# One hand-written order of stages on every engine, in a linear-attention and SoLU kernel

## The chip, the cores and the metric

The kernel runs on one core of a Trainium2 chip. A core has a matrix engine (PE), a vector engine (DVE), an activation engine (ACT), a general engine (POOL), an engine that mostly starts transfers (SP), and 16 DMA engines. Each engine works through its own queue strictly in order, and the engines wait for one another through semaphores. Matrix results land in PSUM, everything else lies in SBUF. The metric is the time of one execution in device microseconds (us).

## What is computed

Two operations run one after the other. The first is a linear attention with a decaying state, for 4 batches, 8 heads, 768 steps and 48 values a head. The second takes its 3072 x 384 result through a two-layer block with a SoLU activation and a layer norm.

```python
for t in range(S):                       # r, k, v, w: (4, 8, 768, 48); u: (8, 48)
    cur = einsum('bhd,bhe->bhde', u[None] * kt, vt)
    y[:, :, t] = einsum('bhd,bhde->bhe', rt, state + cur)
    state = wt[:, :, :, None] * state + einsum('bhd,bhe->bhde', kt, vt)

h = x @ w_in                             # (3072, 384) @ (384, 1024)
sm = softmax(h)                          # over the 1024
solu = h * sm
ln = (solu - mean(solu)) / sqrt(var(solu) + 1e-06) * g_ln
out = ln @ w_out                         # (3072, 1024) @ (1024, 384)
```

## The kernel before

The work is cut into 24 units: 6 chunks of 128 steps, and within each chunk the 4 batches. A unit passes these stages, each a function of the kernel:

- `load`: four tiles (w, k, r, v) of 128 x 384 f32, 192 KB each, started on SP. Each name has 5 buffers.
- `decay`: ACT takes the logarithm of w (tile lw, L128), PE sums it over time into cum_ps (L130, L131), ACT takes the exponential in place (L132).
- `scaled`: DVE forms kp and rp from it (L139, L140). `bonus`: POOL forms vb, p, q and dv, and DVE sums q into dg (L146 to L154).
- `transposed`: PE transposes kp and rp into kr_ps, DVE copies it to kr (L164). `scores`: PE forms m_ps from kr, ACT copies it to m (L176), POOL masks it (L177).
- `attend`: PE sums y_ps from dv, the state st and m times vb; ACT copies it to y (L196). `state`: PE forms s_ps, ACT its decay et (L221), DVE the new st of that batch (L226).
- `x_transposed`: PE transposes y into x_ps, DVE copies it to xT (L235). `hidden`: 24 matmuls form h_ps (L244), ACT takes e = exp(h_ps) (L247), DVE forms he = h_ps * e (L249).
- `output`: 24 matmuls, in eight groups of three, form o_ps (he times w2), g_ps (he times he) and a last column of o_ps (L259 to L262). ACT squares the sums (sq), DVE takes the diagonal of g_ps (junk, L268), POOL subtracts (qm, L270), ACT forms lv, rs and the scaled result o (L272 to L276), and SP stores o.

`setup_weights`, called once, folds the norm's scale and mean into w2: sixteen f32 matmul instructions over w_out and gn (L115), then eight sums on DVE (L119).

The loop at the end of the kernel works on units t, t - 1, t - 2, t - 3 and t - 4 at once. It is not this loop alone that sets the order on the engines: a scheduler moves instructions of different stages past each other by its own estimate of costs, and PSUM and SBUF buffers are handed out in the order that it finds. PSUM has two buffers of tag "b" (cum_ps, m_ps, h_ps), and four of tag "s" (kr_ps, s_ps, x_ps, y_ps, o_ps, g_ps).

Of the kernel before, what the change touches and what calls it, by code (L numbers as in the profile page):

```python
# [16 lines left out]
MULT, ADD = ALU.mult, ALU.add  # L17


@with_exitstack  # L20
def kernel(
# [23 lines left out]
    NU = len(units)  # L45

# [55 lines left out]
    nc.sync.dma_start(out=g_sb, in_=moe_g_ln.rearrange("(ko ki) -> ki ko", ki=128))  # L102
    w2 = consts.tile([128, KF, DM + 1], BF16)

    def setup_weights():

        gr = consts.tile([128, KF], F32)
        nc.vector.tensor_scalar(out=gr, in0=g_sb, scalar1=RDF, scalar2=None, op0=MULT)
        gn = consts.tile([128, KF, 128], F32)
        nc.gpsimd.memset(gn, -1.0 / DF)  # L110
        for f in range(KF):
            nc.vector.tensor_scalar(out=gn[:, f, :], in0=gn[:, f, :], scalar1=gr[:, f:f + 1], scalar2=None, op0=MULT)
        m_ps = small.tile([128, DM], F32, tag="s", name="m_ps")
        for f in range(KF):
            nc.tensor.matmul(m_ps, lhsT=gn[:, f, :], rhs=wout_f[:, f, :], start=(f == 0), stop=(f == KF - 1))  # L115
        m_sb = consts.tile([128, DM], F32)
        nc.vector.tensor_copy(out=m_sb, in_=m_ps)
        for f in range(KF):
            nc.vector.scalar_tensor_tensor(out=w2[:, f, :DM], in0=wout_f[:, f, :], scalar=gr[:, f:f + 1],  # L119
                                           in1=m_sb, op0=MULT, op1=ADD)  # L120
        nc.vector.memset(w2[:, :, DM:], 1.0 / RDF)


    def decay(i):
        L = live[i]
        lw = lw_t[i % NR]
        L["lw"] = lw
        nc.scalar.activation(out=lw[:, :, :D], in_=L["w"], func=LN)  # L128
        cum = big.tile([C, 2, 512], F32, tag="b", name="cum_ps")
        nc.tensor.matmul(cum[:, 0, :DM], lhsT=uti_neg, rhs=lw[:, :, :D], start=True, stop=True)  # L130
        nc.tensor.matmul(cum[:, 1, :DM], lhsT=uts, rhs=lw[:, :, :D], start=True, stop=True)  # L131
        nc.scalar.activation(out=cum[:, :, :DM], in_=cum[:, :, :DM], func=EXP)  # L132
        L["ex"] = cum

    def scaled(i):
# [3 lines left out]
        nc.vector.tensor_mul(out=kp[:, :, :D], in0=ex[:, 0], in1=L["k"])  # L139
        nc.vector.tensor_mul(out=rp[:, :, :D], in0=ex[:, 1], in1=L["r"])  # L140
        L["kp"], L["rp"] = kp, rp

    def bonus(i):
        L = live[i]
        vb = wk.tile([C, H, D], BF16, tag="vb", name="vb")
        nc.gpsimd.tensor_copy(out=vb, in_=L["v"])  # L146
        p = wk.tile([C, H, D], BF16, tag="p", name="p")
        nc.gpsimd.tensor_mul(out=p, in0=L["r"], in1=L["k"])  # L148
        q = wk.tile([C, H, D], BF16, tag="q", name="q")
        nc.gpsimd.tensor_mul(out=q, in0=p, in1=u_bc)  # L150
        dg = wk.tile([C, H], F32, tag="dg", name="dg")
        nc.vector.reduce_sum(out=dg, in_=q, axis=AX)  # L152
        dv = wk.tile([C, H, D], BF16, tag="dv", name="dv")
        nc.gpsimd.tensor_mul(out=dv, in0=vb, in1=dg.unsqueeze(2).to_broadcast([C, H, D]))  # L154
        L["vb"], L["dv"] = vb, dv

    def transposed(i):
        L = live[i]
        kr_ps = small.tile([C, 2 * HP, C], BF16, tag="s", name="kr_ps")
        for j, t in ((0, L["kp"]), (1, L["rp"])):  # L160
            for hp in range(HP):
                nc.tensor.transpose(kr_ps[:, j * HP + hp, :], t[:, 2 * hp:2 * hp + 2, :].rearrange("t a d -> t (a d)"), ident)  # L162
        kr = wk.tile([C, 2 * HP, C], BF16, tag="kr", name="kr")
        nc.vector.tensor_copy(out=kr, in_=kr_ps)  # L164
        L["kr"] = kr

    def scores(i):
# [3 lines left out]
        for hp in range(HP):  # L171
            for a in range(2):
                rows = slice(64 * a, 64 * a + 64)
                nc.tensor.matmul(m_ps[:, a, hp, :], lhsT=kr[rows, hp, :], rhs=kr[rows, HP + hp, :], start=True, stop=True)  # L174
        m = wk.tile([C, 2, HP, C], BF16, tag="m", name="m")
        nc.scalar.copy(out=m, in_=m_ps)  # L176
        nc.gpsimd.affine_select(out=m, in_=m, compare_op=ALU.is_gt, fill=0.0, base=0,  # L177
                                pattern=[[0, H], [1, C]], channel_multiplier=-1)
        L["m"] = m

    def attend(i):
# [4 lines left out]
        nc.tensor.matmul(y_ps, lhsT=ident, rhs=L["dv"].rearrange("t h d -> t (h d)"), start=True, stop=False,  # L186
                         skip_group_check=True)
        if c > 0:
            for hp in range(HP):
                nc.tensor.matmul(y_ps[:, hp * 2 * D:(hp + 1) * 2 * D], lhsT=kr[:, HP + hp, :], rhs=st[:, hp, :],  # L190
                                 start=False, stop=False, skip_group_check=True)
        for h in range(H):
            nc.tensor.matmul(y_ps[:, h * D:(h + 1) * D], lhsT=m[:, h % 2, h // 2, :], rhs=vb[:, h, :],
                             start=False, stop=(h == H - 1), skip_group_check=True)
        y = wk.tile([C, DM], BF16, tag="y", name="y")
        nc.scalar.copy(out=y, in_=y_ps)  # L196
        L["y"] = y

    def state(i):
# [7 lines left out]
        if c > 0:  # L207
            nc.tensor.matmul(s_ps[:, :DM], lhsT=ident, rhs=st.rearrange("p a e -> p (a e)"), start=True, stop=False,
                             skip_group_check=True)
# [12 lines left out]
        sv = s_ps[:, :DM].rearrange("p (a e) -> p a e", a=HP)
        for a in range(2):
            rows = slice(64 * a, 64 * a + 64)
            cols = slice(a * D, (a + 1) * D)
            nc.vector.tensor_mul(out=st[rows, :, cols], in0=sv[rows, :, cols],  # L226
                                 in1=et[rows].unsqueeze(2).to_broadcast([64, HP, D]))

    def x_transposed(i):
        L = live[i]  # L230
        x_ps = small.tile([128, KM, C], BF16, tag="s", name="x_ps")
        for j in range(KM):
            nc.tensor.transpose(x_ps[:, j, :], L["y"][:, j * 128:(j + 1) * 128], ident)
        xT = wk.tile([128, KM, C], BF16, tag="xT", name="xT")
        nc.vector.tensor_copy(out=xT, in_=x_ps)  # L235
# [3 lines left out]
    def hidden(i):  # L239
        L = live[i]  # L240
        h_ps = big.tile([128, KF, C], F32, tag="b", name="h_ps")
        for f in range(KF):
            for j in range(KM):
                nc.tensor.matmul(h_ps[:, f, :], lhsT=win_sb[:, j, f * 128:(f + 1) * 128], rhs=L["xT"][:, j, :],  # L244
                                 start=(j == 0), stop=(j == KM - 1))
        e = wk.tile([128, KF, C], BF16, tag="e", name="e")
        nc.scalar.activation(out=e, in_=h_ps, func=EXP)  # L247
        he = wk.tile([128, KF, C], BF16, tag="he", name="he")
        nc.vector.tensor_mul(out=he, in0=h_ps, in1=e)  # L249
        L["e"], L["he"] = e, he  # L250

    def output(i):
        L = live[i]
        c, b = units[i]
        e, he = L["e"], L["he"]
        o_ps = small.tile([C, DM + 2], F32, tag="s", name="o_ps")
        g_ps = small.tile([C, C], F32, tag="s", name="g_ps")
        for f in range(KF):
            nc.tensor.matmul(o_ps[:, :DM + 1], lhsT=he[:, f, :], rhs=w2[:, f, :], start=(f == 0), stop=False,  # L259
                             skip_group_check=True)  # L260
            nc.tensor.matmul(g_ps, lhsT=he[:, f, :], rhs=he[:, f, :], start=(f == 0), stop=(f == KF - 1))  # L261
            nc.tensor.matmul(o_ps[:, DM + 1:], lhsT=e[:, f, :], rhs=inv_col, start=False, stop=(f == KF - 1),  # L262
                             skip_group_check=True)
        sq = wk.tile([C, 2], F32, tag="sq", name="sq")
        nc.scalar.activation(out=sq, in_=o_ps[:, DM:], func=SQUARE)
        junk = wk.tile([C, C], BF16, tag="junk", name="junk")
        ss = wk.tile([C, 1], F32, tag="ss", name="ss")
        nc.vector.scalar_tensor_tensor(out=junk, in0=g_ps, scalar=1.0, in1=ident, op0=MULT, op1=MULT, accum_out=ss)  # L268
        qm = wk.tile([C, 1], F32, tag="qm", name="qm")
        nc.gpsimd.tensor_sub(out=qm, in0=ss, in1=sq[:, 0:1])  # L270
        lv = wk.tile([C, 1], F32, tag="lv", name="lv")
        nc.scalar.activation(out=lv, in_=sq[:, 1:2], func=LN, scale=1e-6 * DF * DF, bias=qm)  # L272
# [6 lines left out]
    LOOK = 3
    for i in range(2, LOOK):  # L280
        load(i)
    LAST = 5
    for t in range(NU + LAST):
        on = lambda d: 0 <= t - d < NU
        if t + LOOK < NU:
            load(t + LOOK)
        if on(0):
            decay(t)
            bonus(t)
        if on(3):  # L290
            hidden(t - 3)
        if on(0):
            scaled(t)
        if on(1):
            transposed(t - 1)
        if on(2):
            attend(t - 2)
        if on(4):
            output(t - 4)
        if on(1):  # L300
            scores(t - 1)
        if on(2):
            x_transposed(t - 2)
            state(t - 2)
        if t == 1:
            setup_weights()
# [30 lines left out]
```

## Time and profile before

| What | Value |
|---|---|
| median of 3 runs | 202.47 us (201.85 to 202.66) |
| the profiled execution's own time | 202.66 us |
| its span, first to last instruction | 201.0 us |
| busy: PE / DVE / ACT / POOL | 149.8 / 118.7 / 113.3 / 110.3 us |
| moved by DMA | 26.51 MB, of it 101312 packets under 512 bytes |
| DMA engines | 5 to 9 tenths busy in nearly every slice until 150 us, 0 to 2 tenths after, when all loads have landed |

How to read the rows of a profile: a row of the timeline gives the start (us from the span's start), the length, the engine, the line of the kernel, the operation, the tile written and the tiles read, the shape, and in brackets how long the engine stood idle before it and what it waited for. "x24" at the end says that 24 instructions are merged. A matmul's own length overlaps the next one's start, so PE's pace is read from start to start. A row of the busy time by stretches gives the stretch and its length, the busy time of PE, weight loads, DVE, ACT and POOL (with numbers of instructions), the granted PE clock, the DMA engines' busy share and GB/s. In the page's clock row each digit is a fortieth of the span, in tenths of full speed.

### The profile page before, as it was taken

To read this page: it belongs to the slowest core of one execution; us is meant where nothing else is said; L and a number is where in the kernel's file an instruction comes from. 1 tells how busy PE (TensorE), PEld (TensorE's weight loads), DVE (VectorE), ACT (ScalarE), POOL (GpSimd) and SP (SyncE) were. 2 spreads that over 40 slices of the span, in tenths; PEclk is the share of its full clock that TensorE was granted. 3 is DMA by queue.
4 is the path that set the end of the run, shared out by engine and by line. 5 is a ranking of instruction groups with operands and counts; after the bars stand their busy time and mean duration, and the time that the engine had idled before them with its cause. 6 is when DMAs were issued, how large, how long until landed. Compare 5 with 4: busy or idle time off the path is not lost.

```text
span 201.0 us, 5426 instructions
## 1 busy us (share of the span) xinstructions
PE 149.8 (75%) x2144; PEld 117.3 (58%) x2144; DVE 118.7 (59%) x266; ACT 113.3 (56%) x237; POOL 110.3 (55%) x156
## 2 busy tenths in 40 slices
PE   1031394389869797968788988899888988999870
PEld 0010253278757676756676867677776867786650
DVE  3032418959775576668378676777677666663320
ACT  3042103057754775767577677766867677765642
POOL 4046566378754974873986577656865245411200
PEclk9999999559999999999999999999999999999997
DMA  6999799995196799678979597678640111011112
GB/s 115 210 188 297 148 192 186 187 174 109 53 186 151 152 175 205 125 135 171 194 159 159 131 218 151 134 160 175 143 112 10 44 39 42 3 39 42 39 42 80
DMA packets 105946, 26.51 MB, mean 132 GB/s; under 512 B 101312, under 2 KB 105536, under 8 KB 105920
## 3 DMA queue, kind: packets, MB, share of 16 engines
q1 hardware_dynamic: 105520, 25.37, 65.4%
q0 software_dynamic: 400, 0.79, 2.1%
q8 instruction: 17, 0.28, 0.6%
q14 instruction: 9, 0.07, 0.1%
HBM read 22.22 MB, written 4.72 MB: 134 GB/s over the span
## 4 chain that ended last, share of the span: by engine, by line
PE 27%; ACT 15%; issue 14%; DVE 13%; POOL 12%; DMA 11%; SPq 6%; POOLq 0%; DVEq 0%
PE h_ps L244 10%; DMA r_in<-in_r_dram 7%; ACT e L247 6%; SPq L62 5%; DMA g_sb<-in_moe_g_ln_dram 5%; PE o_ps L259 5%; PE m_ps L115 4%; DVE he L249 3%; DVE w L119 3%; POOL m L177 3%; ACT lw L128 3%; DVE junk L268 2%; POOL p L148 2%; POOL q L150 2%; PE cum_ps L130 2%
## 5 line engine op out<-in xcount | busy, mean ns | idle before, releaser
L259 PE MATMUL o_ps<-w,he 128*128 128x385 bf16 x192 | 49.2, 324 | 1.1 <-DVE he L249 1.1
L261 PE MATMUL g_ps<-he 128*128 128x128 bf16 x192 | 41.6, 218 | 0.0
L249 DVE TENSOR_TENSOR he<-h_ps,e 128x1024 bf16<-128x1024 f32 x24 | 29.3, 1221 | 15.8 <-ACT e L247 15.8
L244 PEld LDWEIGHTS <-win_sb 128*128 128x128 bf16 x576 | 35.3, 100 | 4.1 <-issue 1.4
L244 PE MATMUL h_ps<-xT,win_sb 128*128 128x128 bf16 x576 | 37.2, 223 | 0.5 <-ACT m L176 0.5
L262 PE MATMUL o_ps<-inv_col,e 128*128 128x1 bf16 x192 | 31.9, 166 | 0.0
L247 ACT ACTIVATE e<-h_ps 128x1024 bf16<-128x1024 f32 x24 | 24.6, 1023 | 12.5 <-PE h_ps L244 12.4
L270 POOL TENSOR_TENSOR qm<-ss,sq 128x1 f32<-128x1 f32 x24 | 4.5, 190 | 48.5 <-DVE junk L268 48.5
L148 POOL TENSOR_TENSOR p<-r_in,k_in 128x384 bf16<-128x384 f32 x24 | 24.4, 1016 | 9.1 <-DMA r_in<-in_r_dram 9.1
L176 ACT CAST m<-m_ps 128x1024 bf16<-128x1024 f32 x24 | 24.0, 999 | 9.5 <-PE m_ps L174 9.3
L177 POOL TENSOR_SCALAR_AFFINE_SELECT m<-m 128x1024 bf16<-128x1024 bf16 x24 | 26.2, 1091 | 3.9 <-ACT m L176 3.9
L130 PE MATMUL cum_ps<-lw,uti_neg 128*128 128x384 bf16 x24 | 8.2, 343 | 25.0 <-ACT lw L128 25.0
L262 PEld LDWEIGHTS <-e 128*128 128x128 bf16 x192 | 18.4, 96 | 12.5
L139 DVE TENSOR_TENSOR kp<-cum_ps,k_in 128x384 bf16<-128x384 f32 x24 | 13.4, 557 | 20.5 <-ACT cum_ps L132 20.4
L152 DVE TENSOR_REDUCE dg<-q 128x8 f32<-128x384 bf16 x24 | 13.3, 552 | 19.7 <-POOL q L150 15.3
L132 ACT ACTIVATE cum_ps<-cum_ps 128x768 f32<-128x768 f32 x24 | 19.1, 797 | 9.8 <-PE cum_ps L131 7.7
L150 POOL TENSOR_TENSOR q<-p,u_bc 128x384 bf16<-128x384 bf16 x24 | 22.2, 925 | 3.5 <-DMA u_bc<-in_u_dram 1.8
L154 POOL TENSOR_TENSOR dv<-vb,dg 128x384 bf16<-128x384 bf16 x24 | 19.8, 828 | 5.4 <-DVE dg L152 4.3
L164 DVE COPY kr<-kr_ps 128x1024 bf16<-128x1024 bf16 x24 | 16.6, 690 | 8.6 <-PE kr_ps L162 8.3
L128 ACT ACTIVATE lw<-w_in 128x384 bf16<-128x384 f32 x24 | 12.5, 520 | 15.6 <-DMA w_in<-in_w_dram 15.1
L146 POOL CAST vb<-v_in 128x384 bf16<-128x384 f32 x24 | 12.2, 507 | 15.4 <-DMA v_in<-in_v_dram 7.9
L259 PEld LDWEIGHTS <-he 128*128 128x128 bf16 x192 | 18.6, 97 | 1.3 <-DVE he L249 1.2
(61 smaller groups left out, 274.8 us busy)
## 6 DMA issues: line engine op xcount, KB each, us to landing
w_in<-in_w_dram SPq DMA_DIRECT2D x24, 192.0 KB, 4.2
k_in<-in_k_dram SPq DMA_DIRECT2D x24, 192.0 KB, 3.9
r_in<-in_r_dram SPq DMA_DIRECT2D x24, 192.0 KB, 4.1
v_in<-in_v_dram SPq DMA_DIRECT2D x24, 192.0 KB, 4.1
out_dram<-o SPq DMA_DIRECT2D x24, 192.0 KB, 2.0
wout_f<-in_moe_w_out_dram SPq DMA_DIRECT2D x1, 1536.0 KB, 9.7
win_sb<-in_moe_w_in_dram POOLq DMA_DIRECT2D x1, 768.0 KB, 7.8
u_bc<-in_u_dram SPq DMA_DIRECT2D x1, 192.0 KB, 6.3
```

The costliest lines, as they stand in the source:

```text
L132: nc.scalar.activation(out=cum[:, :, :DM], in_=cum[:, :, :DM], func=EXP)
L148: nc.gpsimd.tensor_mul(out=p, in0=L["r"], in1=L["k"])
L150: nc.gpsimd.tensor_mul(out=q, in0=p, in1=u_bc)
L154: nc.gpsimd.tensor_mul(out=dv, in0=vb, in1=dg.unsqueeze(2).to_broadcast([C, H, D]))
L176: nc.scalar.copy(out=m, in_=m_ps)
L177: nc.gpsimd.affine_select(out=m, in_=m, compare_op=ALU.is_gt, fill=0.0, base=0, pattern=[[0, H], [1, C]], channel_multiplier=-1)
L244: nc.tensor.matmul(h_ps[:, f, :], lhsT=win_sb[:, j, f * 128:(f + 1) * 128], rhs=L["xT"][:, j, :], start=(j == 0), stop=(j == KM - 1))
L247: nc.scalar.activation(out=e, in_=h_ps, func=EXP)
L249: nc.vector.tensor_mul(out=he, in0=h_ps, in1=e)
L259: nc.tensor.matmul(o_ps[:, :DM + 1], lhsT=he[:, f, :], rhs=w2[:, f, :], start=(f == 0), stop=False, skip_group_check=True)
L261: nc.tensor.matmul(g_ps, lhsT=he[:, f, :], rhs=he[:, f, :], start=(f == 0), stop=(f == KF - 1))
L262: nc.tensor.matmul(o_ps[:, DM + 1:], lhsT=e[:, f, :], rhs=inv_col, start=False, stop=(f == KF - 1), skip_group_check=True)
```

## The change

Each of PE, ACT, DVE and POOL is wrapped in `InOrder`, which ties every instruction to the one written before it on the same engine. The scheduler can no longer move instructions on these four engines; SP is not wrapped. The stages are cut into a part for each engine (`log_w`, `cumulate`, `decays`, ...), and the new loop writes them out, from t + 1 (logarithm, bonus, cum, scaled) to t - 4 (store). `output` is called in two parts of four groups each. w_in is loaded in f32 through SP ahead of unit 1's tiles and cast on DVE at t = 1; w_out is scaled and centred in bf16 at t = 3, with eight bf16 matmuls and one sum over all of it on DVE. In the profile of the changed kernel nearly all instructions carry the helper's line, L34, so tiles tell them apart.

```diff
+class InOrder:
...
+        def call(*args, **kwargs):
+            if self.last is None:
+                made = make(*args, **kwargs)
+            else:
+                with self.tc.issue_after(self.last):
+                    made = make(*args, **kwargs)
+            self.last = made.ins
+            return made
...
+    pe, act, dve, pool = (InOrder(tc, e) for e in (nc.tensor, nc.scalar, nc.vector, nc.gpsimd))
...
-    load(1)
     u_bc = consts.tile([C, H, D], F32)
     nc.sync.dma_start(out=u_bc, in_=u.partition_broadcast(C))
-    win_sb = consts.tile([128, KM, DF], BF16)
-    nc.gpsimd.dma_start(out=win_sb, in_=moe_w_in.rearrange("(ko ki) f -> ki ko f", ki=128))
+    win_f = consts.tile([128, KM, DF], F32)
+    nc.sync.dma_start(out=win_f, in_=moe_w_in.rearrange("(ko ki) f -> ki ko f", ki=128))
+    load(1)
     wout_f = consts.tile([128, KF, DM], F32)
     nc.sync.dma_start(out=wout_f, in_=moe_w_out.rearrange("(ko ki) d -> ki ko d", ki=128))
...
+    load(2)
...
+    def setup_w_in():
+        for j in range(KM):
+            dve.tensor_copy(out=win_sb[:, j, :], in_=win_f[:, j, :])
+
+    def setup_w_out():
...
+        gw = consts.tile([128, KF, DM], BF16)
         for f in range(KF):
-            nc.vector.tensor_scalar(out=gn[:, f, :], in0=gn[:, f, :], scalar1=gr[:, f:f + 1], scalar2=None, op0=MULT)
-        m_ps = small.tile([128, DM], F32, tag="s", name="m_ps")
+            dve.tensor_scalar(out=gw[:, f, :], in0=wout_f[:, f, :], scalar1=gr[:, f:f + 1], scalar2=None, op0=MULT)
+        m_ps = small.tile([128, DM], F32, tag="s", name="mean_ps")
         for f in range(KF):
-            nc.tensor.matmul(m_ps, lhsT=gn[:, f, :], rhs=wout_f[:, f, :], start=(f == 0), stop=(f == KF - 1))
-        m_sb = consts.tile([128, DM], F32)
-        nc.vector.tensor_copy(out=m_sb, in_=m_ps)
-        for f in range(KF):
-            nc.vector.scalar_tensor_tensor(out=w2[:, f, :DM], in0=wout_f[:, f, :], scalar=gr[:, f:f + 1],
-                                           in1=m_sb, op0=MULT, op1=ADD)
+            pe.matmul(m_ps, lhsT=mean_w, rhs=gw[:, f, :], start=(f == 0), stop=(f == KF - 1))
+        dve.tensor_add(out=w2[:, :, :DM], in0=m_ps.unsqueeze(1).to_broadcast([128, KF, DM]), in1=gw)
...
+    LOOK = 4
+    for t in range(-2, NU + 4):
+        def do(d, *stages):
+            if 0 <= t + d < NU:
+                for stage in stages:
+                    stage(t + d)
+
+        if t > -2 and t + LOOK < NU:
             load(t + LOOK)
...
         if t == 1:
-            setup_weights()
+            setup_w_in()
+        if t == 3:
+            setup_w_out()
+        do(0, bonus_v, transposed, transposed_copy)
+        do(-1, state, state_decay)
+        do(-2, hidden_mul)
+        do(-1, state_update)
+        do(-3, lambda i: output(i, 0))
+        do(-4, store)
+        do(-1, x_transposed, x_copy)
+        do(1, log_w, bonus)
+        do(0, scores, scores_copy, scores_mask)
+        do(1, cumulate, decays)
+        do(-3, lambda i: output(i, 1), squares, sums, centre, scale)
+        do(1, scaled, bonus_sum)
+        do(-1, hidden, hidden_exp)
+        do(0, attend, y_copy)
```

How instructions stand on the engines is best seen in three places. The first is ACT, one unit's round in the steady part of the loop. Before:

```order
L132 ACTIVATE cum_ps<-cum_ps 128x2x384
L247 ACTIVATE e<-h_ps 128x1024
L196 CAST y<-y_ps 128x384
L265 ACTIVATE sq<-o_ps 128x2
L272 ACTIVATE lv<-sq,qm 128x1
L176 CAST m<-m_ps 128x1024
L274 ACTIVATE rs<-lv 128x1
L221 ACTIVATE et<-s_ps 128x4
L128 ACTIVATE lw_95<-w_in 128x8x48
L276 ACTIVATE o<-o_ps,rs 128x384
```

After the change, from the first instruction of an iteration on (names as before):

```order
L34 ACTIVATE et<-s_ps 128x4
L34 ACTIVATE o<-o_ps,rs 128x384
L34 ACTIVATE lw_96<-w_in 128x8x48
L34 CAST m<-m_ps 128x1024
L34 ACTIVATE cum_ps<-cum_ps 128x2x384
L34 ACTIVATE sq<-o_ps 128x2
L34 ACTIVATE lv<-sq,qm 128x1
L34 ACTIVATE rs<-lv 128x1
L34 ACTIVATE e<-h_ps 128x1024
L34 CAST y<-y_ps 128x384
```

The logarithm lw moved from behind sq, lv and m to ahead of them, and e and y now stand last. The second place is PE around the cum matmuls of a steady round. Before:

```order
L190 LDWEIGHTS kr
L190 MATMUL y_ps<-st_112,kr 128x96
L130 LDWEIGHTS uti_neg
L130 MATMUL cum_ps<-lw_95,uti_neg 128x384
L131 LDWEIGHTS uts
L131 MATMUL cum_ps<-lw_95,uts 128x384
L244 LDWEIGHTS win_sb
L244 MATMUL h_ps<-xT,win_sb 128x128
```

After the change (w_145 is the tile w2):

```order
L34 LDWEIGHTS kr
L34 MATMUL m_ps<-kr 128x128
L34 LDWEIGHTS uti_neg
L34 MATMUL cum_ps<-lw_95,uti_neg 128x384
L34 LDWEIGHTS uts
L34 MATMUL cum_ps<-lw_95,uts 128x384
L34 LDWEIGHTS he
L34 MATMUL o_ps<-w_145,he 128x385
L34 LDWEIGHTS he
L34 MATMUL g_ps<-he 128x128
```

Between cum and hidden there now stands the second part of output, and scores stands ahead of cum. The third place is DVE around the setting up of the weights. Before (w_136 is the tile w2):

```order
L152 TENSOR_REDUCE dg<-q 128x8 x2
L108 TENSOR_SCALAR gr<-g_sb 128x8
L112 TENSOR_SCALAR gn<-gn,gr 128x128 x8
L152 TENSOR_REDUCE dg<-q 128x8
L117 COPY m_sb<-m_ps 128x384
L119 SCALAR_TENSOR_TENSOR w_136<-wout_f,gr,m_sb 128x384 x8
L139 TENSOR_TENSOR kp_99<-cum_ps,k_in 128x8x48
```

After the change, at t = 3, followed by the first DVE stages of that iteration as they stand in every later one:

```order
L34 TENSOR_REDUCE dg<-q 128x8
L34 TENSOR_SCALAR gr<-g_sb 128x8
L34 TENSOR_SCALAR gw<-wout_f,gr 128x384 x8
L34 TENSOR_TENSOR w_145<-mean_ps,gw 128x8x384
L34 COPY kr<-kr_ps 128x1024
L34 TENSOR_TENSOR he<-h_ps,e 128x1024
L34 TENSOR_TENSOR st_114<-s_ps,et 64x4x48 x2
L34 COPY xT<-x_ps 128x384
L34 SCALAR_TENSOR_TENSOR junk,ss<-g_ps,ident 128x128
```

The setting up moved from before unit 2's kp to behind unit 3's dg, and in each round the copy kr now stands first, ahead of he, the state and xT.

The order of PSUM buffers of tag "s" is now the same in every round: g_ps takes the buffer that kr_ps of the same iteration had, o_ps that of the last y_ps, and x_ps that of the last o_ps.

More of the change, by code (lines that the diff above doesn't have):

```diff
@@ L17, with __init__, __getattr__ @@
 MULT, ADD = ALU.mult, ALU.add
+class InOrder:
+    def __init__(self, tc, engine):
+        self.tc, self.engine, self.last = tc, engine, None
+    def __getattr__(self, name):
+        make = getattr(self.engine, name)
+        def call(*args, **kwargs):
[6 more added lines that the diff above has]
+            return made
+        return call
 @with_exitstack
@@ L185, in attend @@
         y_ps = small.tile([C, DM], F32, tag="s", name="y_ps")
-        nc.tensor.matmul(y_ps, lhsT=ident, rhs=L["dv"].rearrange("t h d -> t (h d)"), start=True, stop=False,
+        pe.matmul(y_ps, lhsT=ident, rhs=L["dv"].rearrange("t h d -> t (h d)"), start=True, stop=False,
                          skip_group_check=True)
@@ L207, in state @@
         if c > 0:
-            nc.tensor.matmul(s_ps[:, :DM], lhsT=ident, rhs=st.rearrange("p a e -> p (a e)"), start=True, stop=False,
+            pe.matmul(s_ps[:, :DM], lhsT=ident, rhs=st.rearrange("p a e -> p (a e)"), start=True, stop=False,
                              skip_group_check=True)
@@ L243, in hidden @@
             for j in range(KM):
[L244 removed]
+                pe.matmul(h_ps[:, f, :], lhsT=win_sb[:, j, f * 128:(f + 1) * 128], rhs=L["xT"][:, j, :],
                                  start=(j == 0), stop=(j == KM - 1))
[L246 to L248 removed]
@@ L258, in output @@
[L258 to L272, printed above, removed]
@@ L273, in output @@
-        rs = wk.tile([C, 1], F32, tag="rs", name="rs")
-        nc.scalar.activation(out=rs, in_=lv, func=EXP, scale=-0.5)
         o = io.tile([C, DM], F32, tag="o", name="o")
-        nc.scalar.activation(out=o, in_=o_ps[:, :DM], func=COPY, scale=rs)
+        act.activation(out=o, in_=L["o_ps"][:, :DM], func=COPY, scale=L["rs"])
         nc.sync.dma_start(out=out[b * S + c * C:b * S + (c + 1) * C, :], in_=o)
[L279 to L285, printed above, removed]
-            load(t + LOOK)
[L287 to L304, printed above, removed]
-        if t == 1:
-            setup_weights()
+    LOOK = 4
```

160 lines of the change are left out of this document (118 added, 42 removed).

## The prediction

> **What bounds the kernel now.** I read the page's head, then the busy time by stretches, to see whether one engine is full.
>
> ```profile
> span 201.0 us, 5426 instructions
> PE 149.8 (75%) x2144; PEld 117.3 (58%) x2144; DVE 118.7 (59%) x266; ACT 113.3 (56%) x237; POOL 110.3 (55%) x156
> PEclk9999999559999999999999999999999999999997
> ...
> 70.00:100.00 30.00, 24.79 (x380) 19.77 (x378) 18.86 (x42) 19.61 (x42) 19.91 (x27) 1.00 0.87 169
> 100.00:140.00 40.00, 35.60 (x563) 28.88 (x560) 29.75 (x64) 27.80 (x61) 28.01 (x38) 1.00 0.78 159
> ```
>
> None is. For each of the 24 units DVE, ACT and POOL work 4.9, 4.7 and 4.6 us. The DMA engines are 0.87 busy at 169 GB/s and 0.78 at 159, so full they would move 194 to 204 GB/s. The next view is the chain that ended last, in order of time, where it repeats (start, length, what).
>
> ```profile
> 122.36 0.42 ACT lw L128
> 122.83 0.32 PE cum_ps L130
> 123.31 1.35 PE h_ps L244 x24
> 124.69 1.03 ACT e L247
> 126.88 0.30 DVE junk L268 x2
> 127.54 0.29 ACT lv L272
> 128.90 0.42 ACT lw L128
> ```
>
> One unit takes 128.90 - 122.36 = 6.54 us, and the bound is a circle through queues, not an engine: the next unit's lw stands behind an older unit's lv on ACT, that waits for junk, which stands behind he on DVE, that waits for e, and e for the second product's input h_ps, which stands behind cum_ps on PE, and that waits for lw. How much of it is PE's own work is read from the timeline of one such unit, start to start.
>
> ```profile
> 142.44 0.32 PE L130 MATMUL cum_ps<-lw,uti_neg 128*128 128x384 bf16 x1 [0.76 <-ACT lw L128]
> 142.76 1.50 PE L244 MATMUL h_ps<-xT,win_sb 128*128 128x128 bf16 x24
> 144.10 0.36 PE L193 MATMUL y_ps<-vb,m 128*128 128x48 bf16 x8
> 144.30 1.02 ACT L247 ACTIVATE e<-h_ps 128x1024 bf16<-128x1024 f32 x1 [0.55 <-PE h_ps L244]
> 144.31 0.32 PE L259 MATMUL o_ps<-w,he 128*128 128x385 bf16 x1
> 145.22 0.47 ACT L196 CAST y<-y_ps 128x384 bf16<-128x384 f32 x1
> 145.36 1.23 DVE L249 TENSOR_TENSOR he<-h_ps,e 128x1024 bf16<-128x1024 f32 x1 [0.55 <-ACT e L247]
> 146.34 0.40 PE L174 MATMUL m_ps<-kr 64*128 64x128 bf16 x8
> 146.67 0.34 PE L233 MATMUL x_ps<-ident,y 128*128 128x128 bf16 x3
> 146.85 0.33 PE L208 MATMUL s_ps<-st,ident 128*128 128x384 bf16 x1
> 147.28 0.39 PE L162 MATMUL kr_ps<-ident,kp 128*128 128x128 bf16 x4
> 147.36 0.99 ACT L176 CAST m<-m_ps 128x1024 bf16<-128x1024 f32 x1
> 147.73 0.33 PE L186 MATMUL y_ps<-dv,ident 128*128 128x384 bf16 x1
> 147.93 0.69 DVE L164 COPY kr<-kr_ps 128x1024 bf16<-128x1024 bf16 x1 [0.52 <-PE kr_ps L162]
> ```
>
> PE needs cum 0.32, hidden 1.34, output 2.03, scores 0.33, x 0.18, state 0.43, transposes 0.45 and attend 0.54 (its mask part 0.21 by the row, the dv part 0.16 as half of cum, the st part estimated at 0.17 by hidden's pace): 5.62 us. So 0.92 us a unit is waiting.
>
> **The change, the loop of one unit.** I call iteration t's first transpose time 0 and follow the new order. PE: transposes to 0.45, state to 0.88. The kr copy starts at 0.65 (147.93 - 147.28) and ends at 1.34. The first matmul of output's part 0 can start at 0.88, but the first g_ps matmul behind it takes the PSUM buffer of kr_ps, so it waits for the copy: 1.34 and 0.07 of hand-off (an estimate from the gaps between such rows) make 1.41, instead of 1.04. That is a new wait of 0.37. Then the rest of part 0 (half of 2.03 less the first 0.16) to 2.26, x 2.44, scores 2.77, cum 3.09, part 1 to 4.11, hidden 5.45, attend 5.99. **5.99 us** is the loop: 5.62 of PE and 0.37 of waiting.
>
> What else could end later lies before it. The copy is followed by he (to 2.57), which frees the buffer for cum at 2.77. m starts 0.45 behind scores' start, ends near 3.9 and frees hidden's buffer before 4.11. xT is behind he and the two st products, near 3.7, and also before 4.11. lw only waits for a load and stands before m, so the old circle is cut. e starts 1.54 behind hidden's start (144.30 - 142.76), y 0.92 behind e and ends 0.47 later: 7.04, so part 0 of the next iteration, whose buffer y_ps held, may start at 1.1; with the g_ps wait until 1.41 this costs nothing, and would begin to cost 0.15 later. The longest way round ACT and POOL is scores, m, mask, qm, lv, rs, e, y, part 0, x: 0.45 + 0.99 + 0.05 + 1.09 + 0.19 + 0.05 + 0.29 + 0.11 + 0.92 + 0.47 + 0.06 + 1.02 + 0.18 = 5.87, only 0.12 under the loop. The four 192 KB loads and the store of a unit are 0.98 MB, 164 GB/s at 5.99 us, under the 194 to 204 above; SP sends a unit's loads four iterations early, and a store that waits for o on SP holds up loads that have 20 us.
>
> **The change, the start.** Until iteration 3 the loads set the pace. The rows are of POOL, ACT, DVE and the chain.
>
> ```profile
> 25.81 0.99 POOL L148 TENSOR_TENSOR p<-r_in,k_in 128x384 bf16<-128x384 f32 x1 [2.98 <-DMA r_in<-in_r_dram]
> 26.88 0.92 POOL L150 TENSOR_TENSOR q<-p,u_bc 128x384 bf16<-128x384 bf16 x1
> 27.74 0.50 POOL L146 CAST vb<-v_in 128x384 bf16<-128x384 f32 x1
> 30.02 0.99 POOL L148 TENSOR_TENSOR p<-r_in,k_in 128x384 bf16<-128x384 f32 x1 [0.66 <-DMA r_in<-in_r_dram]
> 41.64 1.09 POOL L177 TENSOR_SCALAR_AFFINE_SELECT m<-m 128x1024 bf16<-128x1024 bf16 x1
> 40.91 0.81 ACT L132 ACTIVATE cum_ps<-cum_ps 128x768 f32<-128x768 f32 x1
> 22.88 1.66 DVE L112 TENSOR_SCALAR gn<-gn,gr 128x128 f32<-128x128 f32 x8
> 31.49 6.28 DVE L119 SCALAR_TENSOR_TENSOR w<-wout_f,gr,m_sb 128x384 bf16<-128x384 f32 x8
> 37.69 0.55 DVE L139 TENSOR_TENSOR kp<-cum_ps,k_in 128x384 bf16<-128x384 f32 x1
> 40.23 0.55 DVE L152 TENSOR_REDUCE dg<-q 128x8 f32<-128x384 bf16 x1
> 23.27 7.60 PE m_ps L115 x16
> 41.07 2.73 PE h_ps L244 x24
> ```
>
> The r tile of unit 2 landed at 25.81, of unit 3 at 30.02, 4.2 us later, so a tile takes 1.05 and v of unit 2 lands near 26.9. The same reads from memory stand ahead of it after the change (two units, u, both weights; w_in goes through SP as f32 instead of through POOL's queue), so I keep 26.9, with 2 us to either side. POOL's fixed order puts the mask of unit 1 behind vb, p and q of unit 2: 0.50 + 0.99 + 0.92 + 1.09 end at 30.4. Attend's mask part and hand-off 0.3, transposes to the kr copy 0.65, copy 0.69, he 1.23, cum with its hand-off 0.54, exp 0.81, kp, rp and dg 1.66: DVE is through iteration 2 at 36.3. setup_w_in (three f32 casts of 1024 on DVE) lies in iteration 1 before v of unit 2: even at he's rate for f32 from PSUM, 3.7 us, they are covered by that load; without that cover they would come on top. The two new memsets (mean_w and w2's last column) run while the first loads are under way.
>
> In iteration 3 setup_w_out stands on DVE ahead of the kr copy, and nothing covers it. gw is eight products over 384 elements: gn's 128 took 1.66 / 8 = 0.21 each, the other 256 elements are at least 0.17 (at kr's copy rate, 0.69 for 1024) and at most 0.27 (at he's slope, below), so 0.38 to 0.48 each; f32 in SBUF with one tensor input is nearer to the former, I take 0.41, 3.3 in all. [...] Then the last of eight bf16 matmuls, 0.42 with hand-offs (seven run under gw; the sixteen f32 ones took 7.60), and one sum over 3072 elements out of PSUM: between kp's 384 in 0.55 and he's 1024 in 1.23 an element costs 1.06 ns, so 3.4. With 0.2 for gr 7.3 us, against 7.60 of PE and 6.28 of DVE in a row before. The kr copy of unit 3 then starts at 43.6, so iteration 3 counts from 42.95. PE has idled, and the clock row falls to 5 tenths where it did so before: hidden took 2.73 instead of 1.34. I add 1.4 once (0 to 2.8).
>
> **The sum.** Iteration 4 starts at 42.95 + 5.99 + 1.4 = 50.35, iteration 23 at 50.35 + 19 x 5.99 = 164.15, iteration 24 (no cum in 23) 5.67 later, at 169.8. There hidden of the last unit starts 3.3 in (part 0 at 1.1, x, part 1), then 1.54, e 1.02, he 1.23 and hand-offs: the last output starts at 177.0. Its length to the end is read before:
>
> ```profile
> 193.85 0.34 PE o_ps L259
> ```
>
> 201.0 - 193.85 = 7.15, so the span is 184.1, and with the 1.66 that lie around it (202.66 - 201.0) the execution takes 185.8. The median of the runs is 0.2 under the profiled one: **185.6 us**. The gain of 17 is 0.55 x 20 in the loop and some 6 at the start.
>
> **Rivals.**
> (a) The g_ps wait is hidden (the copy starts earlier, or another buffer is free): PE alone, 5.62, gives 20 x 0.37 = 7.4 less, 178.2. For it: PE's queue is otherwise dense. Against: the buffer is that of kr_ps in every iteration of the new order.
> (b) The way round ACT and POOL, or the loads, ends later: four hand-offs 0.1 longer make 5.87 into 6.3, and 20 x 0.31 gives 191.8. For it: the margin is only 0.12, and a load rate of 156 GB/s would give the same; the busy stretches above run at 159 and 169, though not full.
> (c) The fixed order brings nothing per unit, 6.54 stays, and only the start is won: 20 x 0.55 more, 196.6. Against: lw no longer stands behind lv.
> (d) Slower: PE drops to half clock inside the loop, because each iteration now stops PE between the first o_ps and the first g_ps matmul and again at buffer hand-overs. The 41.07 row prices it: 2.73 / 1.34 doubles PE's 5.62, so 5.6 more for each unit run so; from 3 of 20 units on it eats the 17 us and the kernel is slower (four units: 208). Against: with a wait of 0.76 in every 6.54 us, the clock is 1.00 in both stretches above. [...]
>
> **How the numbers follow.** Less than 0.5%, 1 us, can't be told from no change here. The forecast (182 to 189.5: landing 2, gw 0.6, clock 1.4, loop 0.1 x 20) has 0.53, (a) 0.13, (b) 0.19, (c) 0.08, no difference in the end 0.02, (d) 0.05. So faster 0.93, same 0.02, slower 0.05. The range reaches from (a), 178, to just short of (c), 195, and leaves out about 0.19.
>
> **What will show it.** Hidden to hidden 5.9 to 6.1 us over the middle units; a PE wait near 0.4 for the kr copy in each; no wait of cum for lw beyond the start; DVE's setup row of about 3.4 for w2 with the kr copy behind it near 43 to 45; last output near 177. It is wrong if waits for loads return after 50 us, if the clock row falls below 9 after 55 us, or if m or mask ends after hidden could start.

## The result, and the profile after

| | before | after |
|---|---|---|
| median, us | 202.56 (201.85 to 202.93, 4 runs) | 186.69 (186.17 to 187.83, 4 runs) |
| profiled execution and its span, us | 202.66, 201.0 | 187.83, 186.1 |
| busy PE / DVE / ACT / POOL, us | 149.8 / 118.7 / 113.3 / 110.3 | 151.1 / 120.1 / 113.4 / 108.0 |

The ratio is 0.9228, 95% interval 0.9177 to 0.9279: 7.7% faster. The forecast was 185.6.

The page of after, its head and its clock row:

```profile
span 186.1 us, 5430 instructions
...
PE 151.1 (81%) x2136; PEld 117.1 (63%) x2136; DVE 120.1 (65%) x262; ACT 113.4 (61%) x237; POOL 108.0 (58%) x154
...
PEclk9999999585589999999999999999999999999999
```

The busy time by stretches of after, with the columns of before:

```profile
70.00:100.00 30.00, 29.46 (x459) 23.53 (x458) 22.92 (x51) 23.17 (x51) 22.08 (x31) 1.00 0.90 179
100.00:140.00 40.00, 39.26 (x615) 31.50 (x611) 30.98 (x68) 30.95 (x69) 29.54 (x41) 1.00 0.86 174
```

The work is what it was, within 3 us on each engine; PE's share of the 40 us from 100 on rose from 35.60 to 39.26 at the same full clock. Below is the timeline of one steady round of after, the rows of PE, DVE, ACT and POOL that the prediction's schedule names:

```profile
113.64 0.38 PE L34 MATMUL kr_ps<-ident,kp 128*128 128x128 bf16 x4
114.26 0.47 ACT L34 CAST y<-y_ps 128x384 bf16<-128x384 f32 x1
114.28 0.69 DVE L34 COPY kr<-kr_ps 128x1024 bf16<-128x1024 bf16 x1 [0.50 <-PE kr_ps L34]
114.78 0.32 PE L34 MATMUL o_ps<-w,he 128*128 128x385 bf16 x1
115.03 0.22 PE L34 MATMUL g_ps<-he 128*128 128x128 bf16 x1
115.84 0.33 PE L34 MATMUL x_ps<-ident,y 128*128 128x128 bf16 x3
116.10 0.40 PE L34 MATMUL m_ps<-kr 64*128 64x128 bf16 x8
116.43 0.34 PE L34 MATMUL cum_ps<-lw,uti_neg 128*128 128x384 bf16 x1
116.54 1.01 ACT L34 CAST m<-m_ps 128x1024 bf16<-128x1024 f32 x1 [0.77 <-PE m_ps L34]
116.77 0.33 PE L34 MATMUL o_ps<-w,he 128*128 128x385 bf16 x1
117.63 1.09 POOL L34 TENSOR_SCALAR_AFFINE_SELECT m<-m 128x1024 bf16<-128x1024 bf16 x1 [0.53 <-ACT m L34]
117.75 1.50 PE L34 MATMUL h_ps<-xT,win_sb 128*128 128x128 bf16 x24
119.09 0.33 PE L34 MATMUL y_ps<-dv,ident 128*128 128x384 bf16 x1
119.63 0.38 PE L34 MATMUL kr_ps<-ident,kp 128*128 128x128 bf16 x4
```

From kr_ps to the next kr_ps is 119.63 - 113.64 = 5.99. From the first row, g_ps starts at 1.39 (foretold 1.41), x 2.20 (2.26), scores 2.46 (2.44), cum 2.79 (2.77), part 1 3.13 (3.09), hidden 4.11 (4.11), attend 5.45 (5.45). ACT copies m every 5.99 us from unit 4 (56.68) to unit 20 (152.47): 95.79 / 16.

The chain of after, in order of time, over one round says something else than the prediction:

```profile
113.45 0.91 ACT e L34
114.37 0.38 ACT y L34
...
114.78 0.32 PE o_ps L34
...
116.17 0.35 PE m_ps L34 x8
...
116.54 1.02 ACT m L34
...
117.63 0.65 POOL m L34
...
118.69 0.20 POOL qm L34
...
118.91 0.30 ACT lv L34
...
119.24 0.20 ACT rs L34
...
119.44 0.91 ACT e L34
```

It goes round ACT and POOL: m, mask, qm, lv, rs, e, y, part 0, scores, m. That is the round which the prediction put at 5.87, 0.12 under the loop. But g_ps starts 0.25 after its o_ps (115.03 - 114.78), where the next pair of after, 115.11 and 115.27, has 0.16, and just after the end of the kr copy at 114.97; no row calls it a wait. Both ways are that close, so which of the two sets 5.99 is a question for experiments.

### The profile page after: what moved, and what is told of

Read it like the earlier page. It is cut to its first block, busy times and chain, and to the rows that moved or that the text cites. A ratio compares the mean times of both kernels' runs of the same rounds, so it can differ in the third digit from the quotient of the medians.

```text
span 186.1 us, 5430 instructions
## 1 busy us (share of the span) xinstructions
PE 151.1 (81%) x2136; PEld 117.1 (63%) x2136; DVE 120.1 (65%) x262; ACT 113.4 (61%) x237; POOL 108.0 (58%) x154
## 4 chain that ended last, share of the span: by engine, by line
PE 33%; ACT 29%; POOL 13%; issue 13%; DVE 6%; DMA 3%; SPq 1%; POOLq 0%; DVEq 0%
PE o_ps L34 13%; ACT m L34 9%; ACT e L34 9%; POOL m L34 7%; PE g_ps L34 5%; ACT y L34 4%; PE m_ps L34 4%; PE h_ps L34 4%; DMA u_bc<-in_u_dram 3%; ACT lv L34 3%; PE x_ps L34 2%; DVE gw L34 2%; ACT rs L34 2%; POOL qm L34 2%; DVE w L34 2%
## 5 line engine op out<-in xcount | busy, mean ns | idle before, releaser
L34 PE MATMUL o_ps<-w,he 128*128 128x385 bf16 x192 | 53.9, 331 | 4.7 <-DVE w L34 2.2
L34 PE MATMUL g_ps<-he 128*128 128x128 bf16 x192 | 42.5, 222 | 1.1 <-ACT y L34 1.1
L34 POOL TENSOR_SCALAR_AFFINE_SELECT m<-m 128x1024 bf16<-128x1024 bf16 x24 | 26.2, 1092 | 22.5 <-ACT m L34 22.5
L34 PE MATMUL h_ps<-xT,win_sb 128*128 128x128 bf16 x576 | 38.7, 227 | 0.4 <-ACT m L34 0.2
L34 ACT CAST m<-m_ps 128x1024 bf16<-128x1024 f32 x24 | 24.3, 1011 | 20.4 <-PE m_ps L34 20.4
L34 PEld LDWEIGHTS <-win_sb 128*128 128x128 bf16 x576 | 35.0, 102 | 1.7 <-DVE xT L34 1.1
L34 PEld LDWEIGHTS <-he 128*128 128x128 bf16 x384 | 26.8, 98 | 9.8 <-issue 4.3
L34 POOL TENSOR_TENSOR dv<-vb,dg 128x384 bf16<-128x384 bf16 x24 | 20.3, 847 | 21.8 <-DVE dg L34 20.2
L34 PE MATMUL o_ps<-inv_col,e 128*128 128x1 bf16 x192 | 32.2, 168 | 0.0
L34 DVE TENSOR_TENSOR he<-h_ps,e 128x1024 bf16<-128x1024 f32 x24 | 29.2, 1215 | 4.6 <-ACT e L34 4.6
L34 PEld LDWEIGHTS <-e 128*128 128x128 bf16 x192 | 18.9, 98 | 16.5 <-issue 3.2
L34 ACT ACTIVATE e<-h_ps 128x1024 bf16<-128x1024 f32 x24 | 24.2, 1009 | 4.7 <-PE h_ps L34 4.7
L34 DVE COPY kr<-kr_ps 128x1024 bf16<-128x1024 bf16 x24 | 16.6, 690 | 11.8 <-PE kr_ps L34 11.8
L34 POOL TENSOR_TENSOR p<-r_in,k_in 128x384 bf16<-128x384 f32 x24 | 24.1, 1004 | 0.0
L34 POOL TENSOR_TENSOR q<-p,u_bc 128x384 bf16<-128x384 bf16 x24 | 22.0, 917 | 3.1 <-DMA u_bc<-in_u_dram 1.3
L34 DVE SCALAR_TENSOR_TENSOR junk<-g_ps,ident 128x128 bf16<-128x128 f32 x24 | 7.0, 291 | 22.3 <-PE o_ps L34 22.3
L34 ACT ACTIVATE cum_ps<-cum_ps 128x768 f32<-128x768 f32 x24 | 19.3, 804 | 1.3 <-PE cum_ps L34 1.3
L34 DVE TENSOR_REDUCE dg<-q 128x8 f32<-128x384 bf16 x24 | 13.0, 543 | 8.8 <-POOL q L34 8.8
L34 DVE TENSOR_TENSOR kp<-cum_ps,k_in 128x384 bf16<-128x384 f32 x23 | 12.8, 557 | 8.0 <-ACT cum_ps L34 6.8
L34 POOL CAST vb<-v_in 128x384 bf16<-128x384 f32 x23 | 11.7, 510 | 10.8 <-DMA v_in<-in_v_dram 10.8
L34 ACT ACTIVATE lw<-w_in 128x384 bf16<-128x384 f32 x23 | 11.9, 518 | 9.2 <-DMA w_in<-in_w_dram 9.2
L34 PEld LDWEIGHTS <-kr 64*128 64x128 bf16 (+1 forms) x272 | 11.5, 99 | 8.6 <-DVE kr L34 5.1
```

Source lines behind the costliest of these rows:

```text
L34: made = make(*args, **kwargs)
```

## The experiments

Each is the kernel after with the edit shown, and its ratio is to the kernel before, timed beside it on the same chip (the ratio of after is 0.9228). "Round" is the mean time between ACT's copies of m from unit 4 to unit 20. Two theories stand against each other for the round. K: PE's 5.62 and the wait of the first g_ps matmul for the kr copy. The rival: the way round ACT and POOL, by y. For the start the question is what put iteration 4 some 3 us later than foretold.

### y copied by DVE

```diff
-        act.copy(out=y, in_=y_ps)
+        dve.tensor_copy(out=y, in_=y_ps)
```

> The copy of y_ps to y is done by DVE instead of ACT; nothing else changes. y is then finished about 0.4 us earlier, since it no longer stands behind e. Two theories of what sets the 5.99 us of a round. K (the prediction's): the first g_ps matmul waits for the kr copy, and the way round ACT and POOL to y ends 0.09 us before that; then nothing changes, 5.99 us a round and 186.7 us (186 to 187.5). Y (the chain of the trace, which runs scores, m, mask, qm, lv, rs, e, y, first o_ps matmul): the round falls by up to 0.31 us for the 17 rounds that have a state, to 5.68 us and 181.4 us.

186.29 us, ratio 0.9177 (0.9137 to 0.9218); round 6.00. Taking y off ACT changed nothing per unit, as K said. The timeline of this kernel, PE's first g_ps matmul of a round:

```profile
113.78 0.22 PE L34 MATMUL g_ps<-he 128*128 128x128 bf16 x1 [0.20 <-DVE kr L34]
```

With y out of the way the first o_ps starts earlier and the wait for the kr copy becomes visible.

### g_ps last in part 0

```diff
-            pe.matmul(g_ps, lhsT=he[:, f, :], rhs=he[:, f, :], start=(f == 0), stop=(f == KF - 1))
+            if part == 1:
+                pe.matmul(g_ps, lhsT=he[:, f, :], rhs=he[:, f, :], start=False, stop=(f == KF - 1))
...
+        if part == 0:
+            for f in range(KF // 2):
+                pe.matmul(g_ps, lhsT=he[:, f, :], rhs=he[:, f, :], start=(f == 0), stop=False)
```

> In part 0 of output the four g_ps matmuls are moved behind the four pairs on o_ps, so the first of them comes 0.6 us later and the kr copy is long done; the matmuls and their number are the same. K: the round falls by the 0.09 us by which the kr copy ends after y, to 5.90 us, then y binds; 17 rounds, 185.2 us. Y: no change, 5.99 us and 186.7 us.

185.61 us, ratio 0.9124 (0.9086 to 0.9161); round 5.91. The four g_ps matmuls now stand behind the four pairs into o_ps, past the copy's end. The gain is 0.08, not 0.37, because the way round by y stands just behind: y ends 1.09 after kr_ps (114.26 + 0.47 - 113.64), and part 0 can't start before.

### Both edits

> Both edits, y copied by DVE and the g_ps matmuls of part 0 last. K and Y agree here: neither wait is left, PE works without a stop at 5.65 to 5.70 us a round, 181.4 us (180.5 to 182.5). If the round stays above 5.9 us, both are wrong and a third wait sets it (hidden for the m copy, 0.15 us behind, or cum for he).

181.64 us, ratio 0.8954 (0.8915 to 0.8992); round 5.74. With both ways cut, 0.25 goes, three times the gain of g_last, while y_on_dve alone brought none. So in after the kr copy holds PE, and the way by y lies 0.08 behind it. The 5.65 to 5.70 a round that were expected were missed, while the time lies in its range of 180.5 to 182.5; the timeline of this kernel, the weight load of cum, names what came next:

```profile
117.67 0.10 PEld L34 LDWEIGHTS <-uti_neg 128*128 128x128 bf16 x1 [0.20 <-DVE he L34]
```

Scores started earlier, and cum now waits for its PSUM buffer, which DVE's product `he` frees: from scores to cum 0.42 instead of 0.33 passes.

### The same stages without the fixed order

```diff
-    pe, act, dve, pool = (InOrder(tc, e) for e in (nc.tensor, nc.scalar, nc.vector, nc.gpsimd))
+    pe, act, dve, pool = nc.tensor, nc.scalar, nc.vector, nc.gpsimd
```

> The four wrappers are taken away and the scheduler is free again; the stages are written in the same order, with the same parts, loads and weights. On ACT lw then stands behind rs, o, e and y again. If the fixed order earns the round: 6.4 to 6.6 us a round and 194 to 199 us. If the way that the stages are written and the new start earn it, whoever places the instructions: 5.9 to 6.1 us a round and 185 to 189 us.

191.96 us, ratio 0.9453 (0.9409 to 0.9497): under the 194 expected if the fixed order earns the round, while the round is over its 6.6. ACT's copies of m of units 4 and 20 start at 48.64 and 155.18, 6.66 a round. The same rows of before and of after:

```profile
58.33 0.99 ACT L176 CAST m<-m_ps 128x1024 bf16<-128x1024 f32 x1
...
166.98 0.99 ACT L176 CAST m<-m_ps 128x1024 bf16<-128x1024 f32 x1
```

```profile
56.68 1.01 ACT L34 CAST m<-m_ps 128x1024 bf16<-128x1024 f32 x1 [0.77 <-PE m_ps L34]
...
152.47 1.01 ACT L34 CAST m<-m_ps 128x1024 bf16<-128x1024 f32 x1 [0.77 <-PE m_ps L34]
```

That is 6.79 a round for before (its later rounds 6.54) and 5.99 for after. So cutting the stages and changing the depth brings at most 0.13 a unit; the order, with the PSUM buffers that are handed out by it, brings 0.67. What the free order loses is not the old circle: from 60 to 150 us its profile has no wait of PE for lw. PE's largest wait there is that of g_ps for y, 12 times and 6.2 us in all, so g_ps takes the buffer of y_ps and not that of kr_ps as in after. That cutting the old circle earned the 0.67 is therefore not shown. But unit 4's m is 8 us earlier here than in after (48.64 against 56.68). The timeline of this kernel, DVE's rows of the setup:

```profile
23.44 2.73 DVE L144 TENSOR_SCALAR gw<-wout_f,gr 128x384 bf16<-128x384 f32 x8
35.27 3.35 DVE L148 TENSOR_TENSOR w<-mean_ps,gw 128x3072 bf16<-128x3072 f32 x1
```

The scheduler put gw 14 us earlier than after has it, at a time when POOL was idle, and the sum ends at 38.62. The rows of after, with POOL's and PE's:

```profile
27.76 0.50 POOL L34 CAST vb<-v_in 128x384 bf16<-128x384 f32 x1 [5.81 <-DMA v_in<-in_v_dram]
36.90 0.54 DVE L34 TENSOR_REDUCE dg<-q 128x8 f32<-128x384 bf16 x1
37.53 0.83 POOL L34 TENSOR_TENSOR dv<-vb,dg 128x384 bf16<-128x384 bf16 x1 [1.62 <-DVE gr L34]
37.56 4.97 DVE L34 TENSOR_SCALAR gw<-wout_f,gr 128x384 bf16<-128x384 f32 x8
40.08 0.92 POOL L34 TENSOR_TENSOR q<-p,u_bc 128x384 bf16<-128x384 bf16 x1
43.10 3.36 DVE L34 TENSOR_TENSOR w<-mean_ps,gw 128x3072 bf16<-128x3072 f32 x1 [0.57 <-PE mean_ps L34]
46.37 0.68 DVE L34 COPY kr<-kr_ps 128x1024 bf16<-128x1024 bf16 x1
46.52 0.50 PE L34 MATMUL o_ps<-w,he 128*128 128x385 bf16 x1 [2.18 <-DVE w L34]
51.79 1.73 PE L34 MATMUL h_ps<-xT,win_sb 128*128 128x128 bf16 x24
53.72 0.38 PE L34 MATMUL kr_ps<-ident,kp 128*128 128x128 bf16 x4
```

### The setup earlier, order kept

```diff
-        if t == 3:
-            setup_w_out()
+        if t == 2:
+            setup_centre()
         do(0, bonus_v, transposed, transposed_copy)
...
         do(-1, x_transposed, x_copy)
+        if t == 1:
+            setup_scale()
...
         do(-1, hidden, hidden_exp)
+        if t == 1:
+            setup_mean()
```

Here setup_w_out is cut in three: gr and gw behind the first xT, the mean's matmuls behind the first hidden, the sum at the head of iteration 2; nothing stands in iteration 3.

> The changed kernel with setup_w_out cut in three and put where DVE waits for the loads of unit 2: gr and the eight gw products behind xT of unit 0 in iteration 1, the mean matmuls behind hidden there, the one sum at the head of iteration 2. In the changed kernel the eight products took 4.97 us, the first four 0.90 each while POOL worked on dv, vb, p and q, the last four 0.35 each with POOL idle. If DVE and POOL exclude each other in such an operation: 2.7 to 3.0 us for the eight here, where POOL waits for v of unit 2. If the products are slow for another reason: 4 to 5 us. Either way only the sum, 3.4 us, still delays a round, by about 1.8 us behind dg of unit 2; the kr copy of unit 3 starts near 40 instead of 46.4 and the kernel takes 180.3 us (179 to 182). If the loads set the pace up to unit 5 as well, so that the set-up was partly covered where it stood, less is won: 183 to 185.

179.86 us, ratio 0.8879 (0.8851 to 0.8907); round 5.99 as in after. The timeline of this kernel, DVE's setup and the kr copy of unit 3:

```profile
24.65 2.97 DVE L34 TENSOR_SCALAR gw<-wout_f,gr 128x384 bf16<-128x384 f32 x8
29.98 3.35 DVE L34 TENSOR_TENSOR w<-mean_ps,gw 128x3072 bf16<-128x3072 f32 x1
40.40 0.69 DVE L34 COPY kr<-kr_ps 128x1024 bf16<-128x1024 bf16 x1 [2.12 <-PE kr_ps L34]
```

The kr copy of unit 3 starts at 40.40 instead of 46.37, ACT's copy of m of unit 4 at 48.42 instead of 56.68, and the medians differ by 6.8 (the two profiled executions by 7.9). Of the 8.3 us by which m of unit 4 is earlier, 6.0 are there at the kr copy, and 1.0 of these is not the edit's: v of unit 2 landed at 26.74 here and at 27.76 in after. The other 2.3 come behind the kr copy, where the granted clock in after was 0.50 from 44 to 52 us; its mean over the profiled execution was 0.979 here and 0.952 in after. So the setup's place in iteration 3 cost most of this, through DVE and then through PE, which in after stood 2.18 us for w2 and ran at that clock.

### The setup earlier, and both edits of the round

> The same move of the set-up in the kernel whose y is copied by DVE and whose g_ps matmuls of part 0 stand last (181.6 us). The two gains lie in different stretches, so they add: 175.2 us (174 to 177), 5.74 us a round. If the shorter round then meets the loads, which need 0.98 MB a unit, 171 GB/s: rounds of 5.9 or more with waits for loads, 178 us.

176.59 us, ratio 0.8711 (0.8659 to 0.8763), the best version: 10.1 under after. Alone the edits brought 6.8 and 5.1, together 1.8 less than their sum. The four executions took 175.69, 175.73, 177.46 and 177.70, and the profile is of the slowest, so what it shows need not hold for the two quickest, which are within 0.6 of the 175.2 expected. The timeline of this kernel, gw, shows where part of it went:

```profile
25.90 5.21 DVE L34 TENSOR_SCALAR gw<-wout_f,gr 128x384 bf16<-128x384 f32 x8
```

It starts 1.25 later than in early_alone (y, which DVE copies here, stands ahead of it), so that POOL's vb, p and q (from 27.05 on) fall into it, and takes 5.21 instead of 2.97; the kr copy of unit 3 starts at 43.30 instead of 40.40. Its busy time by stretches:

```profile
100.00:140.00 40.00, 39.84 (x639) 32.38 (x635) 34.97 (x78) 30.15 (x64) 30.85 (x42) 1.00 0.85 167
```

PE is busy 39.84 of 40 us with rounds of 5.74, against 5.62 of its own work.

### Both parts of output where part 0 stood

```diff
-        do(-3, lambda i: output(i, 0))
+        do(-3, lambda i: output(i, 0), lambda i: output(i, 1))
...
-        do(-3, lambda i: output(i, 1), squares, sums, centre, scale)
+        do(-3, squares, sums, centre, scale)
```

> Both parts of output stand where part 0 stood, ahead of x, scores and cum; the rest of the order is the changed kernel's. The kr wait of 0.37 stays, PE's work is the same. Scores then start 1.0 later, so m ends 1.0 later, and hidden, which takes m_ps's buffer, no longer has part 1 of output between: it stands 0.85 us for the m copy. 5.99 + 0.85 = 6.84 us a round, 201 us in all (199 to 203). If the parts bring nothing (the rival: PE does the same work either way): 186 to 188 us.

204.57 us, ratio 1.0091 (1.0066 to 1.0117), 0.9% above the kernel before; round 6.89, where 6.84 was expected, and a time 1.6 above the range given. Part of that miss are the three rounds without state at the end, which grew as well, from 5.74 to 6.73 each. The timeline of this kernel, PE:

```profile
115.03 0.32 PE L34 MATMUL o_ps<-w,he 128*128 128x385 bf16 x1 [0.26 <-ACT y L34]
117.58 0.34 PE L34 MATMUL cum_ps<-lw,uti_neg 128*128 128x384 bf16 x1
118.76 1.50 PE L34 MATMUL h_ps<-xT,win_sb 128*128 128x128 bf16 x24 [0.67 <-ACT m L34]
```

Part 1 was the work under which ACT's m copy ended. Without it hidden waits 0.67 for the PSUM buffer of m_ps; start to start it stands 1.18 behind cum (118.76 - 117.58), 0.86 more than cum's own 0.32, where 0.85 was expected. Part 0 waits 0.26 for y. A cut of one stage in two is worth 0.90 a unit here.

### w_in through POOL's queue, as before

```diff
-    win_f = consts.tile([128, KM, DF], F32)
-    nc.sync.dma_start(out=win_f, in_=moe_w_in.rearrange("(ko ki) f -> ki ko f", ki=128))
...
+    nc.gpsimd.dma_start(out=win_sb, in_=moe_w_in.rearrange("(ko ki) f -> ki ko f", ki=128))
...
-        if t == 1:
-            setup_w_in()
```

> w_in is loaded as before the change, through POOL's queue with the cast in the transfer and behind unit 1's loads on SP; the three DVE casts are gone. The prediction held the casts covered by the wait for v of unit 2, and the bytes ahead of that tile equal: then at most the 0.9 us by which v landed later than forecast comes back, 185.8 to 187 us. If the casts lie on the path, 2.9 us: 183.8 us.

185.57 us, ratio 0.916 (0.9108 to 0.9212), an interval that overlaps that of after: no difference is shown. The median is 0.2 under the range expected if the casts are covered, and 1.8 over what was expected if they are not. The trace of after says the same: DVE's three casts (2.92 us at 20.18) end at 23.10, while POOL's mask of unit 1 starts only at 30.16, behind vb, p and q of unit 2, which began when v landed at 27.76. So the casts lie under the wait for v, as the prediction had it. Here v of unit 2 landed at 25.91 instead of 27.76; but over the kernels in fixed order that load w_in as after does it landed between 26.08 (both) and 27.82 (g_last), so most of this spread is not the edit's, and whether any is stays open.

## Where the prediction was right and where not

- **The loop.** Right: 5.99 foretold, 5.99 measured, and for the reason given: the wait for the kr copy (y_on_dve, g_last and both). The margin of the way round ACT and POOL was 0.08, foretold 0.12. Single starts were off by up to 0.06, so the match to the last hundredth is luck. Rival (a), 5.62, needed only the g_ps wait hidden; g_last hid it and the round was 5.91, for y, and with both ways cut it was 5.74, for cum then waits for `he`. Rival (b) did not come: the loads at 179 and 174 GB/s kept up. Nor did (c), but the argument against it, that lw no longer stands behind lv, is not what decided: in free_order lw stands behind lv again, PE does not wait for lw, and the round is 6.66 all the same.
- **The signs.** Hidden to hidden (5.98, 111.77 to 117.75), the row of 3.36 for w2 and the absence of waits for loads after 50 us came as told. The wait near 0.4 for the kr copy did not show as one: PE stopped 0.27 before the first o_ps, for y, and 0.09 more before g_ps, 0.36 in all. The kr copy behind the setup (46.37) and the last output (178.97) were later than told. Of the last sign, "if m or mask ends after hidden could start", the mask half was mistaken: the mask ended at 118.72, hidden had begun at 117.75, and nothing was lost, since hidden needs only the buffer that the m copy frees (at 117.55).
- **Rival (d), half clock in the loop.** It did not come: 1.00 in both stretches and no clock digit under 9 after 56 us. PE stops for 0.37 in each 5.99 us (5.99 - 5.62), and the clock held beside these stops.
- **The landing of v of unit 2.** 27.76 instead of 26.9; DVE was through iteration 2 at 37.44 (36.90 + 0.54) instead of 36.3: 1.1 late, within the 2 allowed.
- **The step that failed: "I take 0.41, 3.3 in all" for gw.** It took 4.97, outside the 0.38 to 0.48 each. In free_order, with POOL idle, the same eight took 2.73, 0.34 each, and in early_alone, with POOL at work only beside the end of them (from 26.74), 2.97: the price was too high for DVE alone and too low for where it stood. The timeline of after has the first of the eight by itself:

```profile
37.56 1.02 DVE L34 TENSOR_SCALAR gw<-wout_f,gr 128x384 bf16<-128x384 f32 x1
```

The chain of after has the first four:

```profile
37.56 3.67 DVE gw L34 x4
```

That is 0.92 each, just while POOL ran dv, vb, p and q (37.53 to 41.0); the other four share the remaining 1.30, 0.33 each. The forecast priced the operation and never asked what POOL does at that time. In the trace of after the first four products end at 38.58, 39.15, 40.22 and 41.21, each 0.2 behind the end of a POOL instruction (dv 38.36, vb 38.94, p 40.00, q 41.00). early_alone, put at 2.7 to 3.0 if the two engines exclude each other in such an operation, took 2.97, and early_both, with POOL at work from 27.05 on, 5.21 for the same eight. How the two come into each other's way no run shows. The sum out of PSUM (foretold 3.4) took the same beside POOL as without it: 3.36 in after, with POOL idle, and 3.35 in free_order and early_alone, with POOL at work.
- **The half clock.** Iteration 3 from the first o_ps to hidden took 51.79 - 46.52 = 5.27, where a steady round takes 117.75 - 114.78 = 2.97. That is 2.3 in place of 1.4, inside 0 to 2.8; the granted clock was 0.50 from 44 to 52 us, and an o_ps matmul took 0.48 instead of 0.32.
- **The sum.** The kr copy of unit 3 came at 46.37 for 43.6, and iteration 4 began at 53.72 for 50.35: 3.4 late, of it 1.1 landing, 1.6 gw and 0.6 clock and hand-offs. At the end 1.4 came back. The rows of the kernel after, PE in a round without state, and the last output:

```profile
156.70 0.22 PE L34 MATMUL g_ps<-he 128*128 128x128 bf16 x1 [0.38 <-ACT y L34]
...
178.97 0.34 PE L34 MATMUL o_ps<-w,he 128*128 128x385 bf16 x1 [0.43 <-DVE he L34]
```

Units 20 to 23 have no state, so from iteration 21 on there is no s_ps, which the prediction's sum did not count; the buffers of tag "s" go round in another way and g_ps takes that of y_ps. These three rounds took 5.74 (m at 152.47, 158.21, 163.96, 169.70), 0.7 less than three of 5.99, and from m of unit 23 to the last output it was 0.7 shorter than laid out. So the last output started 2.0 late, and with the tail of 7.1 (foretold 7.15) the execution took 187.83 for 185.8. The median was 186.69 for 185.6, since this profiled execution is the slowest of the four. The total was nearer than its parts, by luck: errors of 3.4 and -1.4.
- **Where the gain came from.** By ACT's copies of m, 1.6 us of the 14.9 by which the spans differ were won by unit 4 and 12.9 from there to unit 20. The prediction had some 6 at the start and 11 in the loop: its 6.54 was the late round of before, and over all of units 4 to 20 that kernel took 6.79. That a start worse than foretold met a loop better than foretold is luck too, and early_alone shows that some 6 us more lay in the start.

## What to carry to other kernels

Lay a fixed order out as a schedule: for each matmul of a round write when its operand is there and when the PSUM buffer that it takes comes free, and what lies in between; here that gave the round to 0.01 us, its single starts to 0.06, and named the two edits that took it to 5.74. A stage cut in two is worth what it covers, to be found by putting it back in one place (0.90 us a unit in one_part). One-time work in a fixed order blocks all that stands behind it, so put it where the engine waits for loads (the medians of after and early_alone differ by 6.8 us), and price it by what the engine beside it does at that time (gw took 2.73 us in free_order, 4.97 in after).

## What was not expected of the hardware

- Eight f32 tensor_scalar operations over 384 elements from SBUF on DVE took 2.73 us with POOL idle (free_order), 0.34 each, and 4.97 where POOL worked through half of them (after), 0.92 each beside POOL. The three casts of w_in on DVE took 1.89 us with POOL idle (early_both) and 2.92 beside POOL's mask and dv (after).
- A short wait on a PSUM buffer can stand in no row: g_ps of after started 0.09 behind its pace, without a bracket and off the chain, and with y moved the same matmul shows 0.20 and the kr copy.
- The time at which the same early load landed differed by 1.7 us between kernels that start the same loads in the same order (26.08 and 27.82), one profiled execution of each; whether the kernel or the execution makes the difference is open.
